# Wider copies of the moving vector in the narrow products of a two-layer decode kernel

## The chip, the cores and the metric

The kernel runs on one core of a Trainium2 chip. The metric is the device time of one execution in microseconds, the median of several runs; lower is better. TensorE (PE in the profile) multiplies, PEld is its loading of weights, VectorE is DVE, ScalarE is ACT, GpSimd is POOL, and SyncE (SP) issues nearly all transfers.

## The reference

One token for each of 8 batch rows goes through an attention block, a mixing MLP block, and both again with the same weights and the same cached keys and values. D is 448, there are 16 query heads over 8 key/value heads of 256, and 4096 cached positions.

```python
def _A_ref(x, k_cache, v_cache, wq, wo):
    q = (x @ wq).reshape(B, 1, 16, 256).transpose(0, 2, 1, 3)
    k, v = jnp.repeat(k_cache, 2, axis=1), jnp.repeat(v_cache, 2, axis=1)
    p = _softmax(jnp.einsum("bhqd,bhkd->bhqk", q, k) * 256 ** -0.5)
    o = jnp.einsum("bhqk,bhkd->bhqd", p, v)
    return o.transpose(0, 2, 1, 3).reshape(B, 1, 4096) @ wo

def _B_ref(x, w1, w2, w3, w4):
    h = _gelu(_layernorm(x) @ w1)
    # four quarters of h shifted along the sequence, padded with zeros
    x1 = x + shifted(h) @ w2
    return x1 + _gelu(_layernorm(x1) @ w3) @ w4

x = x + _A_ref(_layernorm(x), k_cache, v_cache, wq, wo)
x = x + _B_ref(_layernorm(x), w1, w2, w3, w4)
x = x + _A_ref(_layernorm(x), k_cache, v_cache, wq, wo)
x = x + _B_ref(_layernorm(x), w1, w2, w3, w4)
```

The sequence has one position, so every shifted quarter is zero and `x1` is `x`: `w1` and `w2` are not needed. What is left of the second block is a layer norm, a product with `w3` (448 to 1792), a GELU and a product with `w4` (1792 to 448).

## The kernel before

The caches are 268 MB of keys and values, and both layers need all of them; 431 MB in all come from HBM, because some tiles are kept from one layer to the next. A tile is the K or the V of one batch row and head, 2 MB; it is loaded in up to four units of 512 KB, and one transfer takes one to four units. On chip there are 30 slots of one unit (`kv`).

For each batch row the program runs the 8 heads of layer 0, the MLP of that row, the 8 heads of layer 1, and the next row's layer 0 is woven into these. A head has a *front* (keys: fp32 transposes of pairs of bf16 values, L1612, then scores by rows, L1503, or, for kept keys, by columns, L1194; a softmax on DVE, POOL and ACT) and a *back* (the weighted sum over V, L1351 in four groups of 512 columns or L1358 in groups of 256; its turn, L1408; the product with `wo`, L1436, L1134 and L1137). A unit's slot becomes free when the last instruction that reads it is done, for V the weighted sum, and only then may SP issue the next transfer into it.

Between the two layers of a row stands `mid`: sums over the row (L807), the first product of the MLP (L966, `h_mms`: 56 matmuls), the nonlinearity on DVE and ACT, the second product (`y_mm`, L1113, and `dup`, L1134 and L1137: 70 matmuls), sums again, and then the queries of layer 1, one head at a time (`second_queries`, through `q_mms`, L950: 16 matmuls each). The first head's queries come at once, the others one after each front of layer 1.

All of these are products of a weight block of 128 x 128 with one column of the activations. The column is streamed many times over (`bcast` repeats it with a step of zero), and each copy writes its own column of PSUM; only one of them is read. The next block's stream begins one column further (or `n` further) and writes over the surplus copies of the one before. How many copies are streamed is set by constants: `QW` and `HW` (32) for queries and first product, `YN` (32) for the second product, `WN` for the product with `wo`, and `COPIES` for the "turned" weighted sums of two of the very last heads (L1368), which stream a pair of probabilities `COPIES` times. In the last MLP, that of two rows, `h_mms` streams pairs of values with `HW // 2` columns. The column sums of `wq` and `w3` (`column_sums`, `column_sums_h`) are made once by the same two functions.

The order of the instructions on every engine is written by a planner in the program (`Plan.schedule`). It goes through all operations with estimated durations and decides which comes next on each engine; where TensorE would stand idle it puts in dummy products with a unit matrix (L1825). `pe(...)` gives an operation's estimated cost by its number of matmuls and its `width`; the emitted instructions need not have that width. The semaphore waits follow from the finished order.

Of the kernel before, what the change touches and what calls it, by code (L numbers as in the profile page):

```python
# [6 lines left out]
P = 128  # L7
B = 8
D = 448
# [37 lines left out]
PV0 = 0  # L47
PV1 = 0
QW, HW, YW = 32, 32, 12
YN = 32  # L50
ON = 14
WN = (28, 24, 12, 12, 12)
SC = 448
YC = 0
ST = 504
# [7 lines left out]
SKIP = 1024  # L63
WOR_AFTER = 100
TURNED = (1, 2)
COPIES = 16
BATCH = 5


# [431 lines left out]
def bass_interleave_layers__gqa_block_cached__mixer_s_mlp__decode_kernel(  # L501
# [43 lines left out]
    w4_sb = sb("w4_sb", [P, 14 * D], bf)  # L545
# [18 lines left out]
    mask = sb("mask", [P, NC5], bf)  # L564
# [155 lines left out]
    def const_c(v):  # L720
# [7 lines left out]
            wr=["sel"])  # L728
# [244 lines left out]
    def column_sums():  # L973

        def one(kc):
            return mask[:, kc:kc + 1]
        for g in range(4):
            pe(lambda t, g=g: q_mms(t, range(8 * g, 8 * g + 8), one, psM, SC, 1, QW), 32,
               rd=["mask"] + WQ, wr=["psM"], banks=[M], prio=len(plan.ops), width=QW)

            dv(lambda v, g=g: v.tensor_single_scalar(
                cs_q[:, 8 * g:8 * g + 8].rearrange("p (h c j) -> p h c j", c=2, j=2),
                psM[:, SC:SC + 8].rearrange("p (h j c) -> p h c j", c=2, j=2), 1.0 / D, ALU.mult),
               rd=["psM"], wr=["cs_q"], banks=[M], prio=len(plan.ops))

    def column_sums_h():
        def one(kc):
            return mask[:, kc:kc + 1]
        pe(lambda t: h_mms(t, one, psM, SC, 1, HW), 56, rd=["mask"] + W3, wr=["psM"], banks=[M],
           prio=len(plan.ops), width=HW)  # L990
        dv(lambda v: v.tensor_single_scalar(cs_h[:, :], psM[:, SC:SC + 14], 1.0 / D, ALU.mult), rd=["psM"], wr=["cs_h"], banks=[M],
           prio=len(plan.ops))
# [43 lines left out]
    def mlp(src, skey, n, dst, dkeys, rows_open=False):  # L1036

        few = n < 3
        ch, kb, bk = where[0]
        at = SC if few else 0  # L1040
        yw, yc, ys = (YN, SC, 1) if few else (BATCH * n, 0, n)
        m = 14 * n
        h_, a_, hT_ = (hb[:, 0:m], g1[:, 0:m], hT) if few else (hb6[:, 0:m], g16[:, 0:m], hT6)
        GK, HK = (["g1"], ["hT"]) if few else (KH, KH)
        if dst is None:
            last_stats(1)
            pe(lambda t: h_mms(t, lambda kc: src[:, kc, 2:2 + n], ch, at, n, HW // 2), 56,
               rd=[*skey] + W3, wr=[kb], banks=[bk], width=HW)
            pe(lambda t: t.matmul(ch[:, at:at + m], ident_f[:, :], t_h[:, :], start=False, stop=True,
                                  skip_group_check=True), 1, rd=["t_h", ("t_h", 1), "ident_f", kb], wr=[kb],  # L1050
               banks=[bk], width=4 * m)
            rows_of_x(src, skey, n)
            for r in range(n):
                ac(lambda a, r=r: a.activation(hb[:, r:m:n], ch[:, at + r:at + m:n], ACT.Gelu_apprx_tanh,
                                               scale=rsy[:, 1, r:r + 1]), 0.25, rd=[kb, "gelu", ("y", 1, B - 2 + r)],
                   wr=["hb"] if r == 0 else [("hb", r)], banks=[bk])
            last_scale(1)
            return last_rows(n)
        elif few:

            c = B - 2
            st, v0, sbank = psR[:, STR:STR + 3], mom[:, 0, c - B + 2:c - B + 3], ["R"]
            if rows_open:
                sums(src, skey, 0, 0, "psM", psM, M)
                st, sbank = mom[:, 2, 0:3], []
                dv(lambda v: v.tensor_copy(st, psM[:, ST:ST + 3]), rd=["psM"], wr=["st"], banks=[M])
            else:
                sums(src, skey, 0, 0, "st")
            for mts in H_PARTS:
                pe(lambda t, mts=mts: h_mms(t, lambda kc: src[:, kc, 0:n], ch, at, n, HW, mts), 4 * len(mts),  # L1070
                   rd=[skey] + W3, wr=[kb], banks=[bk], width=HW)
            variance(st, False, v0, ["st"], "v0", sbank)
            factor(1, c, v0, ["v0"])
            shift(st[:, 2:3], rsy[:, 1, c - B + 2:c - B + 3], ["st", ("y", 1, c)], sbank)
            minus_mean(mom[:, 1, c - B + 2:c - B + 3], st[:, 2:3], ["st"], "mm", sbank)
            dv(lambda v: v.scalar_tensor_tensor(h_, ch[:, at:at + m], rsy[:, 1, c - B + 2:c - B + 3], t_h[:, 0:14],
                                                ALU.mult, ALU.add), rd=[kb, "t_h", ("y", 1, c)], wr=["hb"], banks=[bk])
        else:
            norm(src, skey, True, n)
            pe(lambda t: h_mms(t, lambda kc: yb6[:, kc, 0:n], ch, 0, n, BATCH * n), 56,  # L1080
               rd=KH + W3, wr=[kb], banks=[bk], width=BATCH * n)
            dv(lambda v: v.tensor_copy(h_, ch[:, 0:m]), rd=[kb], wr=KH, banks=[bk])

        HB = ["hb"] if few else KH
        dv(lambda v: v.scalar_tensor_tensor(a_, h_, GELU_C * GELU_K, h_, ALU.mult, ALU.mult),
           rd=HB, wr=GK)
        dv(lambda v: v.scalar_tensor_tensor(a_, a_, GELU_K, h_, ALU.add, ALU.mult),
           rd=HB + GK[:1], wr=GK[:1] + ["a2"])
        plan.op("act", lambda a: a.activation(a_, a_, ACT.Tanh), 0.3, "chain",
                rd=GK[:1], wr=GK[:1], prio=urge[0] + len(plan.ops))  # L1090
        if few:
            factor(0, B - 2, mom[:, 0, 0:1], ["v0"])
            bs = base[:, :, 0]
            dv(lambda v: v.scalar_tensor_tensor(bs, mask[:, :], mom[:, 1, 0:1], src[:, :, 0], ALU.mult, ALU.add),
               rd=["mm", "mask", skey], wr=["base"])
            dv(lambda v: v.scalar_tensor_tensor(bs, bs, rsy[:, 0, 0:1], src[:, :, 0], ALU.mult, ALU.add),
               rd=["base", ("y", 0, B - 2), skey], wr=["base"])
        dv(lambda v: v.scalar_tensor_tensor(hT_[:, 0:m], a_, 1.0, h_, ALU.add, ALU.mult),
           rd=HB + GK[:1], wr=HK)

        def y_mm(t, mts):
            last = None
            for mt in mts:
                for fc in range(14):
                    r = hT_[:, fc * n:(fc + 1) * n]
                    if not few:
                        last = dup(t, ch, yc + mt * ys, yw, w4_sb, fc * D, mt, bcast(r, BATCH, 1), fc == 0, fc == 13)
                        continue
                    a = fc * D + (mt * P if mt < 4 else D - P)
                    if mt == 3 and fc == 13:  # L1110
                        last = dup(t, ch, yc + mt * ys, yw, w4_sb, fc * D, mt, bcast(r, yw, 1), False, True)
                        continue
                    last = t.matmul(ch[:, yc + mt * ys:yc + mt * ys + yw], w4_sb[:, a:a + P], bcast(r, yw, 1),  # L1113
                                    start=(fc == 0), stop=(fc == 13), skip_group_check=(mt == 3))
            return last
        parts = Y_PARTS if few else [range(NC5)]
        for mts in parts:
            pe(lambda t, mts=mts: y_mm(t, mts), 14 * len(mts), rd=HK + W4, wr=[kb], banks=[bk], width=yw)
        ps4 = ch[:, yc:yc + NC5 * ys].rearrange("p (a n) -> p a n", n=ys)
        if few:  # L1120
            yh = ymk[:, :].rearrange("p (a n) -> p a n", n=1)
            dv(lambda v: v.scalar_tensor_tensor(yh, ps4, 0.5, mask[:, :].rearrange("p (a n) -> p a n", n=1), ALU.mult,
                                                ALU.mult), rd=[kb, "mask"], wr=[("acc", 0)], banks=[bk])
            dv(lambda v: v.tensor_tensor(dst, yh, base[:, :, 0:n], ALU.add), rd=[("acc", 0), "base"], wr=dkeys)
            return
        dv(lambda v: v.scalar_tensor_tensor(dst, ps4, 0.5, base6[:, :, 0:n], ALU.mult, ALU.add),
           rd=[kb, "base"] + KH, wr=dkeys, banks=[bk])
# [167 lines left out]
    def back(layer, b, h):  # L1295
# [47 lines left out]
        for u in range(4):  # L1343
# [19 lines left out]
            def pv_turned(t, u=u, q=vs[u]):  # L1363
# [6 lines left out]
                                        bcast(pT[nr][:, k, :], COPIES, 1), start=(u == 0 and s == 0), stop=(u == 3 and s == 7),  # L1370
                                        skip_group_check=True)
                return last
            fn, d = (pv_turned, (0.45, 0.5, 32 * COPIES, 16)) if turned else (pv, (0.25, 0.46, 512, 4 if wide_pv else 8))
            o = plan.op("pe", fn, d, "pv",
                    rd=[("pT", nr, 0), ("pT", nr, 1), ("s", vs[u], 0), ("s", vs[u], 1),
                        "pz"] + [("s", vs[0], 2), ("s", vs[0], 3)] * bool(part and layer and u == 0) + [("acc", 1) if u > 1 else ("o2", 1 - par)] * ((layer, b, h) == (1, B - 1, free_heads[-1]) and u > 0),
# [281 lines left out]
    def second_queries(b, h, prio):  # L1658

        src = x2c[b % 2]  # L1660
        pe(lambda t: q_mms(t, range(4 * h, 4 * h + 4), lambda kc: src[:, kc, 0:1], psM, SC,
                           1, QW), 16, rd=[("x2", b)] + WQ, wr=["psM"], banks=[M], prio=prio, width=QW)
        dv(lambda v: v.scalar_tensor_tensor(
            qz[:, at_q(b, 0):at_q(b, 0) + 64].rearrange("p (c x) -> p c x", c=2)[:, :, 2 * h:2 * h + 2],
            cs_q[:, 4 * h:4 * h + 4].rearrange("p (c j) -> p c j", c=2), mom2[b % 2][:, 2:3],
# [220 lines left out]
```

## Time and profile before

| | |
|---|---|
| three runs | 1063.8, 1066.68 (median), 1069.04 us |
| profiled execution | 1066.43 us, its span 1064.6 us, mean granted TensorE clock 0.985 |
| busy | PE 943.9 us (89%), DVE 595.3 (56%), ACT 354.6 (33%), POOL 98.8 (9%) |
| read from HBM | 430.94 MB, 405 GB/s over the span |
| chain that ended last | DMA 47%, PE 43%, DVE 6% |
| L1612 transposes | 2752 instructions, 372.7 us busy |
| L950 all queries and column sums of `wq` | 1280 instructions |
| L966 first product and column sums of `w3` | 616 instructions |
| L1113 second product | 552 instructions |

The profile cuts the span into 40 slices of 26.6 us and gives for each the busy share of every engine in tenths, the granted TensorE clock, and the rate of the DMA. A matmul's duration in it reaches from its start to its last result, and matmuls are pipelined: a run of them advances by the distance between starts, which is much shorter than a duration. A group of instructions is told by line, engine, operation, what it writes and reads, and shapes: `128*128 128x32 bf16` is a weight block of 128 x 128 and 32 streamed columns.

### The profile page before, as it was taken

What the parts mean: (1) busy time and instruction counts of PE and PEld (TensorE: products, weight loads), DVE (VectorE), ACT (ScalarE), POOL (GpSimd) and SP (SyncE); (2) the same over time, 40 slices, a digit from 0 to 9 for tenths busy, and PEclk for the clock granted to TensorE, in tenths of its full rate; (3) what the DMA queues carried; (4) which work ended last, traced back from release to release, by engine and by line L of the source; (5) the groups of instructions that cost most, each with busy time, mean ns of one, the idle gap of its engine ahead of it and who ended that gap; (6) DMA issues with size and microseconds to landing.
All of it is one profiled execution on the core that took longest, in us unless ns stands there. A gap on an engine that the chain in (4) does not pass through costs nothing.

```text
span 1064.6 us, 31641 instructions
## 1 busy us (share of the span) xinstructions
PE 943.9 (89%) x13915; PEld 651.7 (61%) x13915; DVE 595.3 (56%) x1941; ACT 354.6 (33%) x986; POOL 98.8 (9%) x280
## 2 busy tenths in 40 slices
PE   4889898888989989898898989988899998998898
PEld 4556665566556665566665666656666676666565
DVE  4445555554565545655465655655556665665464
ACT  1234123342233513245132531334314342244142
POOL 0001010010100001001010110101001000111011
PEclk9999999999999999999999999999999999999998
DMA  9999999999999999999999999999999999999995
GB/s 356 410 427 422 411 390 423 428 420 376 396 427 425 416 379 399 426 427 421 391 423 425 425 415 386 426 426 425 412 392 427 425 412 398 407 423 423 383 405 240
DMA packets 56949, 432.99 MB, mean 407 GB/s; under 512 B 6110, under 2 KB 10348, under 8 KB 34796
## 3 DMA queue, kind: packets, MB, share of 16 engines
q1 hardware_dynamic: 56644, 430.59, 98.5%
q8 instruction: 109, 1.79, 0.7%
q10 hardware_dynamic: 168, 0.38, 0.1%
q14 instruction: 28, 0.23, 0.1%
HBM read 430.94 MB, written 0.01 MB: 405 GB/s over the span
## 4 chain that ended last, share of the span: by engine, by line
DMA 47%; PE 43%; DVE 6%; ACT 2%; SPq 1%; issue 1%; POOL 0%; ACTq 0%
DMA kv<-in_A_k_cache_dram 29%; DMA kv<-in_A_v_cache_dram 17%; PE psT L1612 14%; PE psT L1503 6%; PE psP L1351 5%; PE psM L1194 3%; PE psP L1408 2%; PE psP L1358 2%; PE psR L1436 2%; PE psM L950 2%; PE psM L1113 1%; SPq L662 1%; DMA w_sb<-in_B_w_dram 1%; PE psP L1825 1%; DVE kv L1540 1%
## 5 line engine op out<-in xcount | busy, mean ns | idle before, releaser
L1612 PE MATMUL psT<-ident_f,kv 128*128 128x128 f32 x2752 | 372.7, 282 | 22.7 <-DMA kv<-in_A_k_cache_dram 21.0
L1540 DVE COPY kv<-psT 128x512 f32<-128x512 f32 x384 | 264.5, 691 | 179.5 <-PE psT L1612 172.9
L1612 PEld LDWEIGHTS psT<-ident_f,kv 128*128 128x128 f32 x2752 | 302.3, 143 | 99.9 <-issue 56.9
L1541 ACT COPY kv<-psT 128x512 f32<-128x512 f32 x336 | 196.1, 586 | 349.6 <-PE psT L1612 290.9
L1503 PE MATMUL psT<-kv,qz 128*32 128x512 bf16 x1664 | 129.3, 393 | 4.0 <-ACT kv L1541 2.4
L1273 POOL PARTITION_ALL_REDUCE gm<-pm x128 | 45.4, 355 | 757.5 <-DVE pm L1271 689.5
L1351 PE MATMUL psP<-kv,pT 128*4 128x512 bf16 x1376 | 106.8, 378 | 3.5 <-DMA kv<-in_A_v_cache_dram 2.1
L1283 ACT ACTIVATE pT<-pT,gm,fac 128x32 bf16<-128x32 bf16 x128 | 52.6, 417 | 112.5 <-DVE gm L1277 111.7
L1408 PE MATMUL psP<-ident_f,oS 128*128 128x128 f32 x252 | 60.8, 323 | 28.9 <-DVE oS L1397 18.1
L1436 PE MATMUL psR<-wo_sb,oT 128*1 128x192 bf16 (+1 forms) x888 | 66.9, 260 | 13.7 <-DVE oT L1415 11.8
L1408 PEld LDWEIGHTS psP<-ident_f,oS 128*128 128x128 f32 x252 | 39.7, 206 | 53.4 <-DVE oS L1397 35.8
L1289 POOL PARTITION_ALL_REDUCE Db<-rs x128 | 51.0, 398 | 192.5 <-ACT pT L1283 192.5
L1358 PE MATMUL psP<-kv,pT 128*2 128x256 bf16 x1280 | 60.0, 277 | 4.8 <-DMA kv<-in_A_v_cache_dram 4.5
L1503 PEld LDWEIGHTS psT<-kv,qz 128*32 128x32 bf16 x1664 | 31.9, 95 | 46.4 <-issue 12.8
L1283 ACT ACTIVATE pT<-pT,gm 128x32 bf16<-128x32 bf16 x128 | 40.8, 326 | 51.0 <-DVE gm L1277 51.0
L1436 PEld LDWEIGHTS psR<-wo_sb,oT 128*1 128x1 bf16 x888 | 36.8, 82 | 32.8 <-DVE oT L1415 20.3
L1194 PE MATMUL psM<-qz,kv 128*128 128x48 bf16 x1344 | 44.6, 183 | 11.4 <-ACT psM L1323 5.5
L1395 DVE TENSOR_SCALAR oS<-psP,half_rows 128x256 f32<-128x256 f32 x86 | 41.3, 480 | 23.2 <-PE psP L1351 22.9
L1520 DVE CAST sr<-psT 128x512 bf16<-128x512 f32 x53 | 36.6, 691 | 29.0 <-PE psT L1503 28.9
L1351 PEld LDWEIGHTS psP<-kv,pT 128*4 128x4 bf16 x1376 | 30.7, 82 | 34.0 <-issue 10.8
L1194 PEld LDWEIGHTS psM<-qz,kv 128*128 128x128 bf16 x1344 | 38.6, 96 | 21.0 <-DVE kv L1540 7.5
L1266 DVE CAST pT<-psM 128x64 bf16<-128x64 f32 x128 | 28.1, 219 | 39.9 <-PE psM L1194 24.6
(217 smaller groups left out, 945.5 us busy)
## 6 DMA issues: line engine op xcount, KB each, us to landing
kv<-in_A_k_cache_dram SPq DMA_DIRECT2D x69, 2048.0 KB, 23.4
kv<-in_A_v_cache_dram SPq DMA_DIRECT2D x60, 2048.0 KB, 19.9
kv<-in_A_v_cache_dram SPq DMA_DIRECT2D x160, 512.0 KB, 9.5
kv<-in_A_k_cache_dram SPq DMA_DIRECT2D x11, 1536.0 KB, 16.8
kv<-in_A_v_cache_dram SPq DMA_DIRECT2D x15, 1024.0 KB, 9.1
kv<-in_A_k_cache_dram SPq DMA_DIRECT2D x27, 512.0 KB, 8.1
kv<-in_A_v_cache_dram SPq DMA_DIRECT2D x6, 1536.0 KB, 10.3
kv<-in_A_k_cache_dram SPq DMA_DIRECT2D x8, 1024.0 KB, 8.9
```

What stands on the lines that cost most here:

```text
L1194: last = t.matmul(ps[:, SB + 2 * i:SB + 2 * i + 2 * REP], a()[:, c:256:2], bcast(rhs(c), REP, 1), start=(c == 0), stop=(c == 1))
L1273: plan.op("pool", lambda gp: gp.partition_all_reduce(gm[nm][:, :], pm[nm][:, :], P, RO.max), 0.46, "max", rd=[("pm", nm)], wr=[("gm", nm), ...
L1283: return a.activation(sview[:, jj, :], sview[:, jj, :], ACT.Exp, bias=nb[nm][:, jj:jj + 1], scale=scale, accum_out=rs[nr][:, jj:jj + 1])
L1289: plan.op("pool", lambda gp: gp.partition_all_reduce(Db[nr][:, :], rs[nr][:, :], P, RO.add), 0.5, "sum", rd=[("rs", nr, 0), ("rs", nr, 1)] ...
L1351: last = t.matmul(ps[32 * g:32 * g + 4, :], pT[nr][:, k:k + 2, :].rearrange("p k j -> p (k j)"), v, start=(u == 0), stop=(u == 3), skip_gr ...
L1358: last = t.matmul(ps[g4:g4 + 2, PV0:PV0 + DH], pT[nr][:, k, :], slot_ap(q, s * 256, 256), start=(i < 4), stop=(i >= 28), skip_group_check= ...
L1408: last = t.transpose(ps[:, P * c:P * c + P], oS[:, c:DH:2], ident_f[:, :])
L1436: last = t.matmul(psR[r:r + 1, 0:w], oT[no][:, i % 2, i // 2:i // 2 + 1], wo_sb[:, a:a + w], start=(k == 1 and i == 0), stop=(k == turn_at ...
L1503: last = t.matmul(psT[bank][32 * g:32 * g + 32, :], qz[:, a:a + 32], slot_ap(qs[g // 2], g % 2 * 1024, 1024)[:, c:1024:2], start=(half == ...
L1540: return e.tensor_copy(dst, psT[bank][:, :])
L1541: return e.copy(dst, psT[bank][:, :])
L1612: last = t.transpose(psT[bank][:, s * P:(s + 1) * P], src, ident_f[:, :])
```

## The change

More copies are streamed: 48 for the second queries and the column sums of `wq`, 40 for the first product and the column sums of `w3`, 48 for the second product of a single row, 28 for the first product of the last two rows, 36 for the first block of the product with `wo` and of its turn, and 24 pairs, 48 columns, for the turned weighted sums. The planner's estimates keep the old widths, so the order on every engine is the one it had. The PSUM columns that are written stay ahead of the neighbours in use (scores up to column 128, sums from 504).

```diff
 QW, HW, YW = 32, 32, 12
+QX, HX, HL, YX = 48, 40, 28, 48
 YN = 32
-WN = (28, 24, 12, 12, 12)
+WN = (36, 24, 12, 12, 12)
...
-COPIES = 16
+COPIES = 24
...
     column_sums
-            pe(lambda t, g=g: q_mms(t, range(8 * g, 8 * g + 8), one, psM, SC, 1, QW), 32,
+            pe(lambda t, g=g: q_mms(t, range(8 * g, 8 * g + 8), one, psM, SC, 1, QX), 32,
                rd=["mask"] + WQ, wr=["psM"], banks=[M], prio=len(plan.ops), width=QW)
...
     column_sums_h
-        pe(lambda t: h_mms(t, one, psM, SC, 1, HW), 56, rd=["mask"] + W3, wr=["psM"], banks=[M],
+        pe(lambda t: h_mms(t, one, psM, SC, 1, HX), 56, rd=["mask"] + W3, wr=["psM"], banks=[M],
...
     mlp, last two rows
-            pe(lambda t: h_mms(t, lambda kc: src[:, kc, 2:2 + n], ch, at, n, HW // 2), 56,
+            pe(lambda t: h_mms(t, lambda kc: src[:, kc, 2:2 + n], ch, at, n, HL), 56,
...
     mlp, one row
-                pe(lambda t, mts=mts: h_mms(t, lambda kc: src[:, kc, 0:n], ch, at, n, HW, mts), 4 * len(mts),
+                pe(lambda t, mts=mts: h_mms(t, lambda kc: src[:, kc, 0:n], ch, at, n, HX, mts), 4 * len(mts),
...
     y_mm
-                        last = dup(t, ch, yc + mt * ys, yw, w4_sb, fc * D, mt, bcast(r, yw, 1), False, True)
+                        last = dup(t, ch, yc + mt * ys, yx, w4_sb, fc * D, mt, bcast(r, yx, 1), False, True)
...
-                    last = t.matmul(ch[:, yc + mt * ys:yc + mt * ys + yw], w4_sb[:, a:a + P], bcast(r, yw, 1),
+                    last = t.matmul(ch[:, yc + mt * ys:yc + mt * ys + yx], w4_sb[:, a:a + P], bcast(r, yx, 1),
...
     back
-            fn, d = (pv_turned, (0.45, 0.5, 32 * COPIES, 16)) if turned else (pv, (0.25, 0.46, 512, 4 if wide_pv else 8))
+            fn, d = (pv_turned, (0.45, 0.5, 512, 16)) if turned else (pv, (0.25, 0.46, 512, 4 if wide_pv else 8))
...
     second_queries
         pe(lambda t: q_mms(t, range(4 * h, 4 * h + 4), lambda kc: src[:, kc, 0:1], psM, SC,
-                           1, QW), 16, rd=[("x2", b)] + WQ, wr=["psM"], banks=[M], prio=prio, width=QW)
+                           1, QX), 16, rd=[("x2", b)] + WQ, wr=["psM"], banks=[M], prio=prio, width=QW)
```

More of the change, by code (lines that the diff above doesn't have):

```diff
@@ L1040, in mlp @@
         at = SC if few else 0
+        yx = YX
         yw, yc, ys = (YN, SC, 1) if few else (BATCH * n, 0, n)
```

## The prediction

> **What bounds the kernel now.** I read the page first, then stretches of 25 us around the MLPs, then the groups with shapes kept apart, and last the order of time of TensorE where the changed products run. One profiled execution: 1066.43 us, its span 1064.6, so 1.8 us lie around the span; the median of the three runs is 1066.68, so a sum against 1066.43 stands for the median too.
>
> ```profile
> PEclk9999999999999999999999999999999999999998
> DMA  9999999999999999999999999999999999999995
> GB/s 356 410 427 422 411 390 423 428 420 376 396 427 425 416 379 399 426 427 421 391 423 425 425 415 386 426 426 425 412 392 427 425 412 398 407 423 423 383 405 240
> ```
>
> The DMA is busy throughout and moves 423 to 428 GB/s in its good slices. It dips to 376 to 400 once per batch (counted from 0, slices 5, 9, 14, 19, 24, 29, 33, 37), and only the last slice is half empty. So time is lost in the dips, at the start and at the end, and nowhere else. The dips are the MLPs:
>
> ```profile
> core 0: us, PE busy (x) PEld busy (x) DVE busy (x) ACT busy (x) POOL busy (x), PEclk, DMA share, GB/s
> ...
> 262.00:287.00 25.00, 22.30 (x492) 14.93 (x490) 13.14 (x61) 5.42 (x19) 2.26 (x6) 1.00 1.00 376
> 391.00:416.00 25.00, 21.63 (x475) 14.37 (x475) 12.88 (x60) 4.95 (x18) 2.26 (x6) 1.00 1.00 366
> ...
> 300.00:325.00 25.00, 21.31 (x260) 13.74 (x261) 14.15 (x42) 7.30 (x20) 2.26 (x6) 1.00 1.01 425
> ```
>
> The last row is an ordinary stretch (260 matmuls, 425 GB/s); the others, each from an MLP on, hold almost twice the matmuls and about 50 to 60 GB/s less (the dip at 902 us has 398). In those TensorE is the slower one: the DMA queue waits until a product with V (psP, L1358) has freed its slot, and those products stand in TensorE's order between the MLP's. The waits of the DMA queue and the issues between 262 and 274 us say how close that is:
>
> ```profile
> SPq L680 <- PE psP L1358: 109.0, 69, 6.6
> ```
> ```profile
> GB/s 287 396 369 314 314 341 369 382 410 273 218 205 273 273 355 328 355 410 423 423 423 410 423 464 369 362 400 401 370 377 432 416 382 382 328 273 287 328 314 341
> ...
> kv<-in_A_v_cache_dram SPq DMA_DIRECT2D x9, 512.0 KB, 6.9
> ```
>
> A 512 KB transfer issued there lands after a median of 6.9 us; the quickest transfer of this line in the neighbouring stretch 257 to 275 us took 4.9. So a transfer stands about 2 us behind others, and in 0.3 us slices at 205 to 287 GB/s the queue all but runs dry. That 2 us is the cover for whatever makes TensorE later in a dip.
>
> **What a column costs.** The groups, shapes apart (the number after the busy time is the mean ns of one):
>
> ```profile
> L1194 PE MATMUL psM<-qz,kv 128*128 128x48 bf16 x1344 | 44.6, 183 | 11.4 <-ACT psM L1323 5.5 <-DVE oT L1415 2.2 <-DVE qz L1663 2.1
> ...
> L950 PE MATMUL psM<-x2c,wq_sb 128*128 128x32 bf16 x768 | 39.7, 193 | 2.3 <-DVE pT L1266 1.2 <-DVE pm L1271 1.0
> ...
> L1134 PE MATMUL psM<-oT,wo_sb 128*128 128x24 bf16 x68 | 4.5, 183 | 0.0
> L1134 PE MATMUL psM<-oT,wo_sb 128*128 128x12 bf16 x68 | 4.3, 173 | 0.0
> ...
> L1368 PE MATMUL psP<-pT,kv 128*128 128x32 bf16 x128 | 3.9, 176 | 0.0
> ```
>
> L950, L1134 and the MLP's L966 and L1113 stream one value, copied: 12, 24 and 32 columns take 173, 183 and 193 ns. L1194 and L1368 stream a pair of neighbouring values, copied: 32 columns take 176 and 48 take 183. So 48 columns of pairs cost as much as 24 of a single value: a column of a single value costs 0.83 (12 to 24) to 1.0 ns (12 to 32), a column of a pair 0.44. How often one can start follows from a row of the timeline: its length less one duration, over the count less one.
>
> ```profile
> 264.18 0.59 PE L1113 MATMUL psM<-hT,w_sb 128*128 128x32 bf16 x14
> ...
> 265.03 1.44 PE L1113 MATMUL psM<-hT,w_sb 128*128 128x32 bf16 x41
> ...
> 270.51 0.97 PE L1194 MATMUL psM<-qz,kv 128*128 128x48 bf16 x32
> ...
> 1050.95 2.17 PE L1368 MATMUL psP<-pT,kv 128*128 128x32 bf16 x80
> ```
>
> L1113: (590 - 192) / 13 = 30.6 and (1440 - 192) / 40 = 31.2 ns. L1194: (970 - 183) / 31 = 25.4. L1368: (2170 - 176) / 79 = 25.2. There is a floor near 25 ns, pairs lie on it up to 48 columns, and 32 copies of a single value lie 6 ns above it: the stream, not the floor, sets their pace already, at full clock. Further single columns then cost their 0.83 to 1.0 ns each; I take 0.92, the middle.
>
> The Trainium skill, "TensorE: Matmul & The Clock Gate", section "Back-to-back issue gap", gives about 60 cycles (25 ns) for any free size from 1 to 64 once warm. L1194 agrees and L1113 does not (31 ns at 32 columns, clock 1.00). By that page the sum below would be its last term alone.
>
> **The change, part by part.** From 32 to 48 columns is 16 x 0.92 = 14.7 ns each (13.3 to 16), from 32 to 40 is 7.4 (6.6 to 8).
> - Second queries: 768 + 256 = 1024 matmuls (L950), 15.1 us; per head 16, so 0.235 us.
> - Second product of the MLP: 552 + 8 = 560 (L1113 and its half-height one), 8.2 us; per batch 70, 1.03 us.
> - First product: 336 + 112 = 448 (L966), 3.3 us; per batch 56, 0.41 us.
> - Column sums, once: 128 at 14.7 and 56 at 7.4, 2.3 us, at 47 to 53 us and 119 to 121 us, where DMA share is full and transfers issued long before are landing; taken as nothing, at most 2.3.
> - First block of the output product and of its turn, 28 to 36 columns: 100 x 7.4 = 0.7 us, 0.09 per batch.
> - Turned weighted sums (32 to 48) and the last first product (16 to 28) stream pairs; L1194 has 48 columns of pairs at the floor. Nothing.
>
> All of it is 15.1 + 8.2 + 3.3 + 2.3 + 0.7 = 29.6 us of TensorE. Order, waits and DMA issues stay as they are: nothing is moved past a queue. Where TensorE waits for K or V (ordinary stretches), the 4 heads' queries outside the dip fill idle time. In the dip they don't. From the first product on, the next 25 us hold 56, 70 and four times 16 changed matmuls (in the dip at 262 us, queries start at 268.0, 272.8, 279.9 and 284.2): 0.41 + 1.03 + 4 x 0.235 = 2.4 us. Who waits: the V products queued behind, so the slots, so the DMA queue. Against the 2 us of cover I count only half, because the queue is nearly dry in part of the dip: 2.4 - 1.0 = 1.4 us lost per batch, times 8 is 11 us. A lost DMA microsecond isn't given back, since the DMA is at its rate afterwards.
>
> The end works the other way. The profile's clock falls to half in some stretches of 3.41 us, and the last one covers the final products:
>
> ```profile
> 1055.50:1058.90 3.40, 3.14 (x88) 2.46 (x87) 1.10 (x7) 0.36 (x2) 0.24 (x2) 1.00 0.00 0
> 1058.90:1062.30 3.40, 3.09 (x85) 2.23 (x81) 2.20 (x10) 0.73 (x4) 0.74 (x3) 0.51 0.02 5
> ```
>
> Counting columns that TensorE streams (fp32 twice, four side by side once), the stretches before a half-clock one hold 840 to 3120, most others above 2900. The one at 1055.5 has about 2590; wider turned sums and first product add about 850, so the end would run at full clock. The 56 final products (1.48 us at half clock) would save about 0.5 us; nothing to 0.6.
>
> Sum: 11.0 - 0.5 = +10.5, so 1066.4 + 10.5 = 1077 us. Bounds: with all 2 us of cover, 0.4 x 8 - 0.5 = +3; with none, 2.4 x 8 - 0.5 = +19.
>
> **Rivals.**
> 1. The cover holds: +3, 1069. For it: DMA share is 1.00 in the dips, so some transfer is always under way. Against it: they move 366 to 398 GB/s, not 425.
> 2. Single values keep their 31 ns at any width (a fixed price for copying one value): only the end's 0.5 us, 1066. This is what the page's rule would bring. Against it: the duration of such a product grows with its width, by 10 ns from 12 to 24 columns and by 10 more to 32.
> 3. Faster: the wider streams hold the clock. Eight half-clock stretches lie ahead of the last; in each, up to 3.41 / 2 = 1.7 us of TensorE is lost, 13.6 us in all, 1052 with the end. It decides if columns per ns rise: 48 / 31 = 1.55 if the pace stays, against 32 / 31 = 1.03 now. By my pace 48 / 45.7 = 1.05, no denser. Against it too: of those ahead of the end, only the stretch from 994.1 (clock 1.00, then 0.50 from 997.5 on) consists mainly of changed products; others follow waits of TensorE.
> 4. Every added microsecond counts: +29.6 - 0.5, 1095. Against it: the ordinary stretches at 425 GB/s have TensorE waiting for K.
>
> **The numbers.** Forecast 0.63, rival 1 0.14, rival 2 0.08, rival 3 0.08, rival 4 0.07. About 0.5% (5.3 us) is what a measurement of this kernel can tell from no change. Slower by more: forecast and rival 4, 0.70. Within: rivals 1 and 2, 0.22. Faster by more: rival 3, 0.08. The range runs from just below rival 2 (1064.5) to beyond the forecast's uncovered end of 1085 (1090), leaving rivals 3 and 4 out.
>
> **What would show it.** Right: L950 and L1113 with 48 columns at some 207 ns, a row of 41 at 41 x 46 instead of 1.44 us (about 2.0), L1194 and the 48-column L1368 still at 25 ns, the same transfers in the same order, GB/s in the MLP slices lower by some 10, the other slices as now. Wrong in its first step: a row of 41 still at 1.44 us. Wrong in its second: longer rows, but the dips at the same GB/s and the span within 5 us. The end: PEclk 9 in the last slice and L1023 in about 0.9 us. Wrong altogether: fewer half-clock stretches and shallower dips.

## The result, and the profile after

The changed kernel takes 1077.6 us, the median of six runs (1073.0 to 1079.7), against 1067.4 (1063.0 to 1069.0): a ratio of 1.0100, 95% interval 1.0080 to 1.0121. That is 10.2 us slower. Its profiled execution took 1075.13 us with a span of 1073.3, so 8.7 us more of span than before.

The page of the changed kernel (clock, DMA share and rate by slice of 26.8 us):

```profile
PEclk9899899999999999999999999999999999999999
DMA  9999999999999999999999999999999999999995
GB/s 362 408 427 422 409 381 426 425 423 396 386 424 424 421 367 412 425 426 419 358 422 427 423 415 351 426 425 427 399 362 427 423 414 403 388 424 420 380 410 227
```

The good slices are as good as before (422 to 427). The dips have become deeper: 358, 351 and 362 stand where 391, 386 and 392 stood. Stretches of 25 us of the changed kernel, one from each MLP on, cut at the same places of a batch row as the prediction's, relative to the second product; the last line is the ordinary stretch:

```profile
core 0: us, PE busy (x) PEld busy (x) DVE busy (x) ACT busy (x) POOL busy (x), PEclk, DMA share, GB/s
132.00:157.00 25.00, 24.40 (x475) 16.66 (x475) 11.96 (x50) 5.28 (x18) 2.26 (x6) 1.00 0.98 374
261.00:286.00 25.00, 22.51 (x456) 15.52 (x456) 12.05 (x55) 5.04 (x18) 1.86 (x5) 1.00 0.97 365
390.00:415.00 25.00, 22.71 (x467) 15.78 (x467) 12.80 (x58) 4.86 (x18) 1.86 (x5) 1.00 0.97 357
520.00:545.00 25.00, 24.09 (x479) 16.10 (x472) 13.43 (x56) 4.91 (x19) 2.26 (x6) 1.00 0.97 368
650.00:675.00 25.00, 24.08 (x481) 16.68 (x480) 12.91 (x55) 4.86 (x18) 2.49 (x7) 1.00 0.98 364
779.00:804.00 25.00, 23.52 (x479) 16.75 (x481) 13.43 (x56) 5.04 (x19) 2.26 (x6) 1.00 0.98 360
909.00:934.00 25.00, 24.71 (x486) 16.94 (x484) 13.88 (x56) 5.20 (x18) 2.61 (x7) 1.00 0.99 377
1008.00:1033.00 25.00, 24.03 (x424) 17.33 (x423) 16.57 (x74) 9.11 (x25) 2.26 (x6) 1.00 0.99 372
...
300.00:325.00 25.00, 21.49 (x262) 13.98 (x263) 14.85 (x44) 7.28 (x20) 2.26 (x6) 1.00 1.00 425
```

The six dips of the kernel before that the prediction doesn't show:

```profile
133.00:158.00 25.00, 23.58 (x494) 15.44 (x495) 12.82 (x53) 5.91 (x19) 2.61 (x7) 1.00 1.00 386
...
519.00:544.00 25.00, 23.75 (x496) 15.43 (x492) 14.20 (x62) 4.91 (x19) 2.39 (x7) 1.00 1.02 399
647.00:672.00 25.00, 23.36 (x493) 16.18 (x493) 13.56 (x57) 5.86 (x21) 2.61 (x7) 1.00 1.01 394
773.00:798.00 25.00, 23.41 (x490) 15.52 (x486) 14.06 (x59) 5.00 (x19) 2.26 (x6) 1.00 1.01 392
902.00:927.00 25.00, 24.06 (x500) 16.01 (x501) 14.31 (x58) 5.84 (x21) 2.61 (x7) 1.00 1.01 398
1000.00:1025.00 25.00, 23.55 (x425) 16.31 (x422) 16.49 (x73) 9.07 (x25) 2.26 (x6) 0.98 1.00 376
```

The DMA share in a dip is 0.97 to 0.99, where it was 1.00 to 1.02: some of the DMA engines now stand idle for short times. The ordinary stretch moves 425 GB/s as it did. Over all eight dips the mean rate is 367.1 GB/s, against 385.9 before; 18.8 GB/s over 25 us are 0.47 MB, which take 1.1 us at 425 GB/s, and eight times that is 8.8 us. By this count the dips hold the loss of the span, but not evenly: 1.9 us of it lie in the first three, 6.7 in the fourth to the seventh, 0.2 in the last.

The wait that grew is the one that the prediction named, that of the DMA queue for the products with V that free a slot (L1360 now), 109.0 us in 69 waits before:

```profile
SPq L681 <- PE psP L1360: 119.2, 70, 6.5
```

That is 10.2 us more; no other wait of the DMA queue is more than 3 us longer. In the profiles of the experiments that wait goes with the time: 116.8 to 123.4 us in the kernels that lost 0.5% or more, 111.4 in the one that lost 0.4%, 105.3 to 109.4 in those level with the kernel before, with one exception (113.5 with 32 columns of pairs).

The groups (mean ns of one after the busy time) and TensorE's order of time:

```profile
L951 PE MATMUL psM<-x2c,wq_sb 128*128 128x48 bf16 x768 | 52.5, 206 | 1.3 <-DVE pT L1268 1.2
...
L1196 PE MATMUL psM<-qz,kv 128*128 128x48 bf16 x1344 | 44.6, 183 | 11.4 <-ACT psM L1325 5.5 <-DVE oT L1417 2.2 <-DVE qz L1665 2.1
...
L967 PE MATMUL psM<-x1c,w_sb 128*128 128x40 bf16 x336 | 18.7, 200 | 0.0
```
```profile
263.02 0.78 PE L1115 MATMUL psM<-hT,w_sb 128*128 128x48 bf16 x14
...
264.05 1.98 PE L1115 MATMUL psM<-hT,w_sb 128*128 128x48 bf16 x41
...
1059.55 3.36 PE L1370 MATMUL psP<-pT,kv 128*128 128x48 bf16 x80
...
1069.53 0.86 PE L1024 MATMUL psM<-w_sb,hb 128*2 128x112 bf16 x56
```

Two groups with 48 columns of the same shape stand side by side: copies of one value (L951) take 206 ns, copies of a pair (L1196) 183. The row of 41 went from 1.44 to 1.98 us: (1980 - 206) / 40 = 44.4 ns from start to start, where it was 31.2. The median distances between starts over the whole execution are 44 ns (48 columns of a single value), 37 (40 columns) and 25 (48 columns of a pair at full clock). In the turned sums from 1059.55 on, where the granted clock was 0.50 (1059.3 to 1062.7 us), the pair takes 40.

### The profile page after: what moved, and what is told of

Its sections match the earlier page's. It is cut to its first block, busy times and chain, and to the rows that moved or that the text cites. A ratio compares the mean times of both kernels' runs of the same rounds, so it can differ in the third digit from the quotient of the medians.

```text
span 1073.3 us, 31641 instructions
## 1 busy us (share of the span) xinstructions
PE 967.7 (90%) x13915; PEld 679.2 (63%) x13915; DVE 597.6 (56%) x1941; ACT 355.2 (33%) x986; POOL 98.8 (9%) x280
## 4 chain that ended last, share of the span: by engine, by line
PE 67%; DMA 19%; DVE 8%; ACT 2%; issue 2%; SPq 1%; POOL 0%; POOLq 0%; ACTq 0%; DVEq 0%
PE psT L1614 23%; DMA kv<-in_A_k_cache_dram 14%; PE psT L1505 8%; PE psP L1353 7%; DMA kv<-in_A_v_cache_dram 5%; PE psM L951 4%; PE psR L1438 4%; PE psP L1410 4%; PE psM L1196 3%; PE psP L1360 3%; PE psM L1115 2%; PE psP L1827 2%; PE psM L967 2%; DVE oS L1397 1%; ACT kv L1543 1%
## 5 line engine op out<-in xcount | busy, mean ns | idle before, releaser
L1360 PE MATMUL psP<-kv,pT 128*2 128x256 bf16 x1280 | 58.5, 275 | 1.3 <-DMA kv<-in_A_v_cache_dram 0.8
L1196 PE MATMUL psM<-qz,kv 128*128 128x48 bf16 x1344 | 44.6, 183 | 11.4 <-ACT psM L1325 5.5
L951 PE MATMUL psM<-x2c,wq_sb 128*128 128x48 bf16 x768 | 52.5, 206 | 1.3 <-DVE pT L1268 1.2
L1196 PEld LDWEIGHTS psM<-qz,kv 128*128 128x128 bf16 x1344 | 38.6, 96 | 21.2 <-DVE kv L1542 7.5
L951 PEld LDWEIGHTS psM<-x2c,wq_sb 128*128 128x128 bf16 x768 | 45.6, 98 | 10.0 <-DVE pT L1268 5.7
## 6 DMA issues: line engine op xcount, KB each, us to landing
kv<-in_A_v_cache_dram SPq DMA_DIRECT2D x60, 2048.0 KB, 18.8
```

Of the source, the lines that this page charges most:

```text
L951: last = t.matmul(bank[:, at + i * step:at + i * step + copies], w, r, start=(kc == 0), stop=(kc == 3))
L1196: last = t.matmul(ps[:, SB + 2 * i:SB + 2 * i + 2 * REP], a()[:, c:256:2], bcast(rhs(c), REP, 1), start=(c == 0), stop=(c == 1))
L1360: last = t.matmul(ps[g4:g4 + 2, PV0:PV0 + DH], pT[nr][:, k, :], slot_ap(q, s * 256, 256), start=(i < 4), stop=(i >= 28), skip_group_check= ...
```

## The experiments

Every ratio is to the kernel before, on the same chip in turn, with its 95% interval. Theory A: copies of a value that is not stored beside its twin cost more time per column than copies of a pair, and TensorE's delay in the dip starves the DMA once a small cover is used up. Theory B: every added microsecond of TensorE counts, wherever it lies. Theory C: not the pace matters, but where the clock falls to half.

### The parts one at a time

Each edit stands against the changed kernel.

```diff
-QX, HX, HL, YX = 48, 40, 28, 48      # COPIES = 24, WN[0] = 36
+QX, HX, HL, YX = 32, 32, 16, 48      # e1, COPIES = 16, WN[0] = 28
+QX, HX, HL, YX = 48, 32, 16, 32      # e2, the same
+QX, HX, HL, YX = 32, 40, 16, 32      # e3, the same
+QX, HX, HL, YX = 32, 32, 28, 32      # e4, COPIES = 24, WN[0] = 28
```

Second product alone: 

> Only the second product of the MLP streams 48 copies; everything else is as before. Theory A (a copied single value costs some 0.8 ns per column, and what is added in the dip after an MLP starves the transfers once a cover of 1 us is used up): L1115-type rows go from 31 to 44 ns each, 560 x 13 = 7.3 us of TensorE, 0.9 us per batch, all of it early in the dip; 1 to 5 us slower than before. Theory B (every added microsecond of TensorE counts, wherever it is): 7 us slower. Theory C (not the pace, but where the clock falls to half makes the difference): the same rows at 44 ns, but within 1 us of before unless the number of half-clock stretches differs.

Second queries alone: 

> Only the second queries and the column sums of wq stream 48 copies. 1024 x 13 = 13.3 us of TensorE in the queries, 1.7 in the sums; of the queries four heads of eight, 0.8 us per batch, lie in the dip. Theory A: 2 to 6 us slower, since half of it lies where TensorE waits for keys. Theory B: 15 us slower. Theory C: within 1 us.

First product alone: 

> Only the first product of a single row and the column sums of w3 stream 40 copies: 31 to 37 ns, 448 x 6.3 = 2.8 us, 0.35 us per batch, at the head of the dip. Theory A: 0 to 2 us slower, the least of the three parts. Theory B: 3 us. Theory C: within 1 us.

Pairs alone: 

> Only the products that stream pairs are widened: the turned weighted sums to 48 and the last first product to 28 columns. Theory A: they stay at 25 ns where the clock is full; within 1.5 us of before, faster by up to 0.5 if the last stretch runs at full clock, slower by up to 1.2 if the turned sums fall into a half-clock stretch (40 ns each there, as in the changed kernel's profile). Theory B: no difference. Theory C: this part holds what the clock can bring, so any difference of the whole change, 10 us, would be found here.

Measured: second product 1.0051 (1.0029 to 1.0073), 5.4 us; second queries 1.0014 (0.9994 to 1.0035); first product 1.0002 (0.9982 to 1.0022); pairs 0.9987 (0.9965 to 1.0010). By the measured distances the queries add the most TensorE time (13.6 us, against 7.4 for the second product), and by the middle of the intervals they cost about a quarter of what the second product does. So "every microsecond counts" (B) falls with this one run: it asked for 15 us. The clock theory (C) falls with the pair parts, which hold none of the 10 us. The wider first block of the product with `wo` stands in no run by itself; it is in the changed kernel and in the one without pair parts below. Without it, the second product and the first four queries (below) already cost 0.90%.

### The same columns, as pairs

The first four lines put the edit in words.

```diff
-hT[fc] written once; x1c, x2c = [x, 1, -1]
+hT[2 * fc : 2 * fc + 2] written twice; x1c, x2c = [x, x, 1, -1]
-bcast(r, copies, 1)            # r one value
+bcast(r, copies // 2, 1)       # r the pair
+QX, HX, HL, YX = 48, 40, 16, 48      # e5; COPIES = 16, WN[0] = 28
+QX, HX, HL, YX = 32, 32, 16, 32      # e6; the same
```

> The vector that is copied is stored twice side by side (hT, x1c, x2c), so that second queries, first and second product of a single row stream 24, 20 and 24 copies of a pair: 48, 40 and 48 columns as in the change, with the same values in them. Other widths as before. Theory A (the price is per value that isn't paired with its neighbour): these rows start every 25 ns at full clock instead of 44 and 37, 6 ns less than before; TensorE has 12 us less than before, 1.1 us per batch in the dip; level with before to 8 us faster. Rival (the price is per streamed column of a narrow product, or a copy costs as such): 37 to 44 ns and slower by 5 us or more, as the change without its last parts.

> The same pairs with 32 columns throughout (16 pairs). Theory A: 25 ns at full clock and 27 at half clock, where 48 columns take 40; 0 to 8 us faster than before, within 2 us of the 48 columns of pairs. If the wider pairs hold the clock better, that one is ahead of this one. Rival: 31 ns as before, and the time of before.

Measured: 0.9989 (0.9973 to 1.0006) with 48, 40 and 48 columns, 0.9996 (0.9983 to 1.0009) with 32. In the queries and both products the first of them streams as many columns as the change, with the same values, and the whole loss is gone. Its order of time, groups, and stretches:

```profile
262.95 1.20 PE L1120 MATMUL psM<-hT,w_sb 128*128 128x48 bf16 x41
```
```profile
L954 PE MATMUL psM<-x2c,wq_sb 128*128 128x48 bf16 x768 | 34.9, 184 | 1.4 <-DVE pT L1273 1.2
...
L954 PE MATMUL psM<-ms,wq_sb 128*128 128x48 bf16 x96 | 6.2, 206 | 0.3 <-DVE pT L1273 0.3
```
```profile
515.00:540.00 25.00, 22.81 (x484) 14.40 (x485) 13.60 (x60) 4.91 (x19) 2.26 (x6) 1.00 1.01 393
645.00:670.00 25.00, 23.86 (x512) 16.14 (x512) 14.87 (x61) 6.23 (x22) 3.01 (x8) 1.00 1.01 392
770.00:795.00 25.00, 22.02 (x485) 14.52 (x485) 13.85 (x62) 5.00 (x19) 2.26 (x6) 1.00 1.01 390
```

The row of 41 takes 1.20 us, (1200 - 183) / 40 = 25.4 ns, shorter than before the change. In one group list of one kernel, 48 columns of the same weights take 184 ns from a pair (the queries) and 206 from a single value (the column sums, whose vector was left single): the price goes with the number of separate values or pairs, and columns as such were free up to 48 at full clock. The dips are back at a DMA share of 1.00 to 1.02. But TensorE now has 5 to 6 ns less per product than before, 10 to 12 us in all, and the time is that of before within the interval. The dips move 391.2 GB/s on the mean, 5 more than before, and not the 425 of the ordinary stretch: so something besides the pace of these products keeps them low, and what it is no run shows.

### What the delay is worth, and where

```diff
+QX, HX, HL, YX = 48, 40, 16, 32      # e13; COPIES = 16, WN[0] = 28
+QX, HX, HL, YX = 48, 40, 16, 48      # e15; COPIES = 16, WN[0] = 36
+QX, HX, HL, YX = 32, 32, 16, 48      # e10, e11; COPIES = 16, WN[0] = 28
+copies = 48 if q_count[b] <= 4 else QX      # e10: a row's first four queries
+copies = 48 if q_count[b] > 4 else QX       # e11: its last four
```

> Second queries and first product widened, second product as before: the complement of the second product alone. If parts share one cover (alone they cost 0.14% and 0.02%): 2 to 5 us slower than before, more than 1.7 us, the sum of the two alone. If costs simply add: 1.7 us.

> The change without the two parts that stream pairs (turned sums at 32 and last first product at 16 columns); wider single values as in the change. Theory A: the change plus the 0.13% that the pair parts alone gained, 10 to 13 us slower than before. If the turned sums cost the change 1 us in its profile by falling into a half-clock stretch: 9 to 10 us slower.

> Second product at 48 copies, and of a row's eight second queries only the first four that are made (those in the dip) at 48; the rest and everything else as before. Theory A, with the cover used up by the second product (which alone cost 0.51%): the first four add 0.83 us per batch in the dip, most of it uncovered, so 4 to 6 us more than the second product alone: 9 to 12 us slower than before. If place makes no difference, this and its twin below are level.

> Second product at 48 copies, and only the last four of a row's second queries at 48: as much TensorE as in its twin above, but later. Theory A: they lie where TensorE is waiting for keys, so little more than the second product alone: 5 to 7 us slower than before. Level with the twin if place makes no difference.

The second column is worked out from the measured distances at full clock (on the mean 13.3 ns more per product of a query or of the second product, 6.6 per first product), with four of eight heads' queries in the dip:

| widened | TensorE added per row in the dip, us | ratio (95%) | per row, us |
|---|---|---|---|
| first product | 0.37 | 1.0002 (0.9982 to 1.0022) | 0.0 |
| queries | 0.85 | 1.0014 (0.9994 to 1.0035) | 0.2 |
| second product | 0.9 | 1.0051 (1.0029 to 1.0073) | 0.7 |
| queries, first product | 1.2 | 1.0038 (1.0020 to 1.0057) | 0.5 |
| second product, first four queries | 1.8 | 1.0090 (1.0075 to 1.0105) | 1.2 |
| second product, last four queries | 0.9 | 1.0076 (1.0058 to 1.0095) | 1.0 |
| all single values | 2.15 | 1.0106 (1.0074 to 1.0137) | 1.4 |

The last column is the ratio less one, times 1066 us, over eight rows; it is a mean, and the rows don't share it evenly (see the part on the prediction). The smallest delay costs nothing and 2.15 us cost 1.4. Most rows fit a cover of some 0.6 to 0.8 us and nearly one for one beyond it. Two don't: the second product loses 0.7 of its 0.9 us, and with the last four queries 1.0. So one cover, the same for any delay in the dip, isn't shown. Queries and first product together cost 0.38%, where alone they came to 0.16; as a cover used by both would have it, though the intervals are too wide to show it. The last four queries were expected to be hidden, 5 to 7 us in all, and came out at 8.1 (6.2 to 10.1); their interval overlaps both that of their twin and that of the second product alone. So that the place within a row matters is not shown by this pair. What speaks for it is that the queries alone cost so little, and the unchanged 425 GB/s of the ordinary stretch.

### Delay without width

```diff
 for mt in mts:
+    for k in range(6 if few else 0):    # the first six once more, then written anew
...
+        t.matmul(ch[...], w4_sb[...], bcast(hT_[:, k:k + 1], yx, 1), start=(k == 0), stop=(k == 5))
     for fc in range(14):
+QX, HX, HL, YX = 32, 32, 16, 32      # e12; COPIES = 16, WN[0] = 28
```

> As before, all widths 32, but each of the five blocks of the second product first streams six of its matmuls once more into the columns that it then writes anew: 30 matmuls of 31 ns more per batch, 0.93 us, as much as 48 copies add to it. Theory A (delay of TensorE in the dip is what costs): as the second product at 48 copies alone, 3 to 7 us slower than before. Theory C (something of the width itself, columns or clock): no slower than 1 to 2 us, since no product is wider.

Measured: 1.0103 (1.0076 to 1.0130), 11 us. No product is wider, and the slowdown is there, so delay alone is enough. But it is twice that of the second product at 48 copies, and I expected 3 to 7. The added time on TensorE is the same: in the second dip the second product takes 4.03 us from its first start to its last, 4.01 with 48 copies and 3.09 before. The kernel has 480 more instructions for it (a weight load and a matmul each); in its profile the second dip is far deeper than the others (355 to 369 GB/s), and partly at half clock:

```profile
262.00:287.00 25.00, 21.35 (x480) 14.99 (x480) 9.96 (x55) 3.61 (x11) 1.11 (x3) 0.84 0.89 308
395.00:420.00 25.00, 22.77 (x518) 15.78 (x522) 13.66 (x67) 4.66 (x17) 1.86 (x5) 1.00 0.97 357
```

By the starts of the same products, the profiled run fell back 4.3 us in that dip against the kernel before, the second product at 48 copies 1.0. But that run took 1079.4 us, 2.7 more than the median of its kernel, and the half clock need not stand there in the others. Why it costs twice as much is not settled.

### Pairs everywhere

```diff
+QX, HX, HL, YX = 48, 40, 28, 48      # e14: values stored twice as in e5, COPIES = 24, WN[0] = 28
```

> Everything that streams copies streams pairs: values stored twice for second queries and both products of a single row (48, 40, 48 columns), turned sums at 48, last first product at 28; product with wo as before. The two halves alone came to 0.9989 and 0.9987 of before. If they add: 0.9976, 2 to 3 us faster than before. If a dip without TensorE's delay is bound by the transfers themselves, not more than that.

Measured: 0.9989 (0.9970 to 1.0008). It is 1% below the changed kernel's ratio and cannot be told from the kernel before. The gains of e4 and e5 did not add; each was within its uncertainty.

## Why the prediction was right, step by step

- **The pace of a single value.** Forecast 14.7 ns more at 48 columns and 7.4 at 40; measured on the mean 13.3 and 6.6, the low ends of the stated 13.3 to 16 and 6.6 to 8. The slope is that of the step from 12 to 24 columns (0.83 ns), not the steeper one that I averaged in. The Trainium skill, "TensorE: Matmul & The Clock Gate", section "Back-to-back issue gap", with its 25 ns for 1 to 64 columns, holds for pairs at full clock (25 ns) and not for single values (44 ns at 48 columns); for those the measurement decides.
- **Pairs free.** Right at full clock, where the 48-column turned sums and score products start every 25 ns. I left out the half clock: there 48 columns of pairs take 40 ns, and a half-clock stretch fell on 80 of the turned sums in the changed kernel's profile, 3.36 us instead of 2.17.
- **What counts is the dip.** The loss lies in the eight dips (8.8 us of a span 8.7 longer), the DMA queue waits longer where the prediction said, and the ordinary stretch is unchanged. That the *later* queries are hidden in it is open. The sign of "some 10 GB/s" less was too small: it was 18.8 on the mean, and 1.4 us lost of 25 would itself have asked for about 24.
- **The cover.** 1.0 us of the 2.4 was taken off. With the delay as measured, 2.15 us, and 1.1 us lost per row in the profile, it is 1.05; by the table's medians 0.6 to 0.8 for most rows, and 0.2 for the second product alone. That 1.0 came so near is luck. The 4.9 us, from which the 2 us of cover were taken, belong to a transfer of 116 KB; the quickest of 512 KB in that stretch took 5.3 us, which leaves 1.6 us of cover, and the half of it that the prediction counts is 0.8. The halving itself had no measurement behind it. So added time and cover were both a little too large, and the errors cancel.
- **Even over the rows.** Wrong. From the first to the eighth dip the rate fell by 12, 11, 9, 31, 30, 32, 21 and 4 GB/s. The four dips that were deepest before (366 to 386 GB/s: the first three and the last) fell by 4 to 12, the four others (392 to 399) by 21 to 32, and all eight stand at 357 to 377 now. The starts of TensorE's products say the same, since both kernels run the same 13915 in nearly the same order: set against the same product before, the changed kernel is 0.3 us late at 516 us, ahead of the fourth dip, and 8.6 at 1050 us. For the second product alone it is 1.4 us ahead and 4.8 late, with the first four queries 0.8 ahead and 7.7 late, with the last four 1.8 ahead and 9.3 late, for all single values 3.3 and 14.6 late. All are measured against one execution of the kernel before; against the mean of it and three of the level kernels (queries, first product and pairs alone) the changed kernel is 1.6 us late at 516 us and 8.3 at 1050. So 1.4 us times 8 had about the right total and the wrong shares: 0.1 to 0.6 us in each of the first three rows, 1.4 to 1.9 in each of the next four, and little in the last. No run explains why.
- **The end.** The 56 final products did run at full clock: 0.86 us against 1.48. But the half-clock stretch had moved onto the turned sums and cost 1.2 us there, so in this profile the end lost where 0.5 us of gain was forecast. The kernel without widened pairs also had its final products at 0.86 us: where that stretch falls varies without those widths, and my count of columns doesn't decide it.
- **Rivals.** A fixed price per copy (rival 2) falls with the 44 ns, a held clock (rival 3) with a mean granted clock of 0.982 against 0.985, every microsecond (rival 4) with the queries alone. Rival 1, a cover that holds, fits the queries and the first product by themselves, which cannot be told from no change.

## What to carry to other kernels

Before widening a stream because columns look free, find two groups of one width whose streamed operands are laid out differently, and compare their durations: here 48 columns at full clock cost 25 or 44 ns, depending only on whether the value was stored twice, side by side. Added time on an engine that isn't the bottleneck is priced stage by stage: look where the transfers it releases land soonest after issue, measure how much cover is left there, and expect little loss below it and, as here, 1.4 of 2.15 us beyond. A saving isn't the reverse of a delay: 10 to 12 us less of TensorE brought nothing that could be measured here.

## What the runs showed of the hardware

- At full clock a bf16 matmul whose streamed values are a repeated single value starts every 31 ns at 32 columns, 37 at 40 and 44 at 48; from a repeated pair it is 25 ns at 32, 40 and 48 columns. The single value's pace at 32 and 40 columns is the same at half clock (31 and 37 ns); the pair's is not: 27, 34 and 40 ns at 32, 40 and 48 columns there (the kernels with 32 and with 48 columns of pairs, and the turned sums of the changed kernel).
- Storing the value twice brings back the 25 ns at full clock, for the same result and the same number of columns.
- Durations follow the number of separate values or pairs: 24 single values (24 columns) and 24 pairs (48 columns) both take 183 ns.
